# Both halves of a block's values in one place, and the value loads right behind it: an attention and feed-forward kernel on one Trainium2 core

## The chip, the cores and the metric

The kernel runs on one core of a Trainium2 chip. The metric is the device time in microseconds, the median of the runs. One execution was also taken by the hardware profiler; its page and its trace are quoted below. Engines are named as there: PE is TensorE's matrix multiplication and PEld its weight load, DVE is VectorE, ACT is ScalarE, POOL is GpSimd, SP is SyncE, which here only issues DMA transfers.

## The reference

Eight batches of attention with twelve heads, 448 positions and 64 values per head. Two 12 x 12 matrices mix the heads, one ahead of the softmax and one behind it. A feed-forward layer with a gate of its own follows. All in fp32.

```python
scores = scale * np.matmul(q, k.transpose(0, 1, 3, 2))
scores = np.einsum('bhij,hg->bgij', scores, w_pre)
scores = scores - np.max(scores, axis=-1, keepdims=True)
attn = np.exp(scores)
attn = attn / (np.sum(attn, axis=-1, keepdims=True) + 1e-09)
attn = np.einsum('bhij,hg->bgij', attn, w_post)
attn_out = np.matmul(attn, v)              # (8, 12, 448, 64)
x = attn_out.transpose(0, 2, 1, 3).reshape(3584, 768)
h = x @ w_in                               # 768 -> 2048
out = (h - np.tanh(h)) @ w_out             # 2048 -> 768
```

## The kernel before

The kernel has two stages. The first, some 940 us of the profiled execution, is the attention; beside it the weights of the feed-forward layer, which arrive as pairs of 32-bit words, are converted in small steps (`narrow_steps`, 56 chunks) and stored to DRAM (`ws`). The second stage is the feed-forward layer, and the change does not touch it.

**Blocks and places.** A batch's 448 positions are cut into four blocks of 120, 120, 120 and 88, so there are 32 blocks. A block is worked off in groups of ten positions times twelve heads (120 rows), which makes 45 groups in a batch and 360 in all. The main loop takes two groups at a time; each round is a *place* `p`, and there are 180. Every place does the following, in this order on TensorE:

- `premix(p)` (L504 to L509): mixes the heads of the scores of two groups, into `ps_p`. The first group is multiplied in fp32, the second in three passes of split operands (`th`, `tl`).
- jobs that the table `todo[p]` lists: `prep_k` (L407, transposes keys), `prep_q` (L433, transposes queries), `values` (L586, attention times values), `scores` (L467, queries times keys).
- `mix(p - 1)` (L549): the second mixing of heads for the two groups of the place before, into `ps_o`.

Beside that, DVE takes the maxima (`mx`, L519) and ACT the exponentials (`e`, L521) of the place; ACT scales `wpost` by the sums (`wr`, L537) and copies the mix of the place before from PSUM into the tile `at` (L558, L565). `scores` leave as `s` (L473, three copies on ACT, one on DVE); two places later SP's `gather` (L488) brings groups of them as `t` into the shape that `premix` needs. POOL and DVE split `t` (L496, L497).

**Values.** `values(i, t)` multiplies block `i` for six heads, half `t` of 0 and 1. Its 24 matmuls run as pairs in the two column halves of the array (`j * D`), over four chunks of keys. The result leaves by DVE copies (L604) into the tile `x`, and behind the second half of every other block SP stores `x` to DRAM (`xs`). The values of a batch come in three loads of four heads (`vr`, three buffers, `load_v`); half 0 reads the first and a part of the second, half 1 the rest. All of `prep_k`, `prep_q`, `values` and `scores` take their PSUM banks from one pool of four, `ps_m`: one bank for each job of the first three kinds, four for a pair of `scores`.

**What sets the order.** On each engine the instructions run in the order in which the program is written (`in_order`). The table is filled ahead of the loop: a list `halved` has, for each block, three jobs of scores ("s", four heads each) and two of values ("v"), each with its earliest and latest place; one is put into each place, the one that is due first, and kinds take turns if that makes nobody late. A block's values can begin two places after its last group's. `prep_q` stands one place ahead of the scores that need it. `load_k` and `load_v` go into the places at fixed distances from a block's start. A load that is put into a place is issued by SP at the beginning of the next one, behind that place's two gathers (`issue`); the stores of converted weights (`ws`) and the loads of the next chunk (`cr`) come after these, in the same SP queue.

Of the kernel before, what the change touches and what calls it, by code (L numbers as in the profile page):

```python
# [148 lines left out]
def kernel_body(  # L149
# [179 lines left out]
    with ExitStack() as st:  # L329
# [377 lines left out]
        NG = len(groups)  # L707
# [5 lines left out]
        NPL = NG // 2  # L713
# [8 lines left out]
        def at_place(p, *job):  # L722
            todo[p].append(job)

        halved = []
        for i in range(len(blocks)):

            f0, f1, f2 = first[i : i + 3]
            if i + 1 < len(blocks):
                lo = max(0, (f0 - 1) // 2 - 1)  # L730
                hi = f1 // 2 - 3
                for x in range(0 if i else 1, 3):
                    e = lo + 2 * x if lo + 4 <= hi else lo + (hi - lo) * x // 2
                    halved.append((e if i else x - 1, hi, "s", i + 1, x))
            for x in range(2):
                halved.append(((f1 - 1) // 2 + 2, f2 // 2 + 1 if f2 < NG else NPL + 7, "v", i, x))
        at_s, p, kind = {}, 0, None
        while halved:
            ready = sorted((x for x in halved if x[0] <= p), key=lambda x: (x[1], x[3:]))
            if ready:  # L740
                x = ready[0]
                assert p <= x[1], (p, x)

                other = [y for y in ready if y[2] != kind]
                if x[2] == kind and other and x[1] > p + 1:
                    x = other[0]
                halved.remove(x)
                _, _, kind, i, n = x
                if kind == "s":
                    at_s[i, n] = p  # L750
                    for hp in (2 * n, 2 * n + 1):
                        at_place(p, scores, i, hp)
                else:
                    at_place(p, values, i, n)
            p += 1
        for i, (b, m) in enumerate(blocks):
            p0 = first[i] // 2
            if i + 2 < len(blocks):
                p = at_s[i + 2, 0] - 1
                at_place(p, prep_q, i + 2, 0)  # L760
                at_place(p, prep_q, i + 2, 1)
                if i + 3 < len(blocks):
                    at_place(p + 1, load_q, i + 3)
            if b and m == 0:
                for hq in range(NP // 2):
                    at_place(p0 + 4 + hq, load_v, b, hq)
        for b in range(1, B):
            p, o, done = first[blocks.index((b - 1, 1))] // 2 - 1, 0, []
            for hq in range(3):
                if hq == 2:  # L770

                    p = max(p, done[0] + 1)
# [81 lines left out]
    for n in range(N):  # L854
        b, f = n // NF, n % NF
# [49 lines left out]
```

## Time and profile before

| | us |
|---|---|
| median of 3 runs | 1884.85 (1882.71 to 1889.16) |
| the profiled execution | 1890.93 |
| its span, first to last instruction | 1889.2 |

| in the profiled execution | |
|---|---|
| mean granted TensorE clock | 0.996 |
| DMA over the span | 371.92 MB, mean 197 GB/s |
| a value load (`vr`) | 24 of 448.0 KB |
| a key load (`kr`) | 23 of 448.0 KB |
| a gather (`t`) | 342 of 210.0 KB, 16 of 189.0 KB on SP |
| a store of attention output (`xs`) | 8 of 720.0 KB, 8 of 624.0 KB |

Times in the lines of the profile are microseconds from the span's start unless marked ns. In rows of the timeline the first number is the start and the second the length of the merged run of like instructions; an fp32 matmul of the program stands there as two instructions. In rows of groups the numbers behind the first bar are busy time and mean ns of one, and behind the second the idle time of the engine just before them and what ended it. In rows of waits the numbers are us in total, times, and the longest. SPq is SP's queue of DMA issues. Lengths of matmuls overlap, so starts are compared rather than lengths.

### The profile page before, as it was taken

How to read it: one execution, taken by the hardware profiler on the slowest of the kernel's cores; microseconds unless marked ns; L12 is line 12 of the kernel's file. 1: busy time of each engine (PE TensorE's matmuls, PEld its weight loads, DVE VectorE, ACT ScalarE, POOL GpSimd, SP SyncE). 2: the span in 40 equal slices, each digit the busy share in tenths (PEclk: the TensorE clock that was granted, in tenths of full speed). 3: DMA queues.
4: the chain of work that ended last, by engine and by line, in shares of the span. 5: the costliest groups of instructions: out<-in, count | busy, mean ns of one | idle time of the engine just before them, and what ended most of it. 6: DMA issues, size and time to landing. Idle time of an engine off the chain costs nothing.

```text
span 1889.2 us, 35293 instructions
## 1 busy us (share of the span) xinstructions
PE 1856.8 (98%) x13122; PEld 1525.3 (81%) x13122; DVE 1187.3 (63%) x2462; ACT 1136.4 (60%) x2510; POOL 455.3 (24%) x401
## 2 busy tenths in 40 slices
PE   8999999999999999999999999999999999999998
PEld 5777887777877787877788888888888888888887
DVE  5676766767776676766456556556556556556555
ACT  5787887878888788788633433443443443443433
POOL 1344444444444345444200000000000000010000
PEclk8999999999999999999999999999999999999999
DMA  6667658676575857656565566555655655655650
GB/s 150 182 186 207 188 164 220 182 199 198 176 217 168 207 180 207 191 162 195 204 259 211 197 227 215 212 213 207 215 213 209 218 214 202 220 214 199 216 198 34
DMA packets 232219, 371.92 MB, mean 197 GB/s; under 512 B 98928, under 2 KB 206960, under 8 KB 217712
## 3 DMA queue, kind: packets, MB, share of 16 engines
q1 hardware_dynamic: 231740, 369.24, 60.4%
q8 instruction: 104, 1.70, 0.4%
q14 instruction: 67, 0.55, 0.1%
q10 hardware_dynamic: 308, 0.43, 0.1%
HBM read 245.37 MB, written 47.19 MB: 155 GB/s over the span
## 4 chain that ended last, share of the span: by engine, by line
PE 87%; DMA 5%; ACT 3%; issue 1%; DVE 1%; SPq 1%; POOL 0%; ACTq 0%; DVEq 0%; POOLq 0%
PE ps_o L549 14%; PE ps_h L260 8%; PE ps_h L256 8%; PE ps_h L255 8%; PE ps_m L586 7%; PE ps_q L467 6%; PE ps_p L504 6%; PE ya L299 5%; PE ya L302 5%; PE ya L300 5%; DMA t<-s 3%; PE yb L300 3%; PE yb L302 3%; PE yb L299 3%; PE ps_p L508 2%; PE ps_p L507 2%
## 5 line engine op out<-in xcount | busy, mean ns | idle before, releaser
L549 PEld LDWEIGHTS ps_o<-wr,e 120*112 120x112 f32 (+1 forms) x2880 | 307.2, 177 | 50.7 <-issue 29.9
L549 PE MATMUL ps_o<-wr,e 120*112 120x120 f32 (+1 forms) x2880 | 340.5, 271 | 4.8 <-ACT wr L537 4.8
L519 DVE TENSOR_REDUCE mx<-ps_p 120x1 f32<-120x448 f32 x360 | 218.8, 623 | 139.1 <-PE ps_p L504 139.0
L497 POOL TENSOR_TENSOR tl<-t,th 120x448 fp32r<-120x448 f32 x179 | 204.8, 1144 | 392.0 <-DVE th L496 258.9
L287 ACT CAST gh<-r 128x512 fp32r<-128x512 f32 (+1 forms) x113 | 69.7, 617 | 378.2 <-DVE r L280 378.2
L256 PE MATMUL ps_h<-xl,w 128*128 128x512 f32 x672 | 263.8, 393 | 0.5 <-POOL pad L222 0.5
L255 PE MATMUL ps_h<-xh,w 128*128 128x512 f32 x672 | 263.8, 393 | 0.0
L521 ACT ACTIVATE e<-ps_p,mx 120x448 f32<-120x448 f32 x360 | 226.0, 637 | 34.7 <-DVE mx L519 34.2
L245 POOL TENSOR_TENSOR xl<-rx,xh 128x512 fp32r<-128x512 f32 x38 | 56.5, 1488 | 742.5 <-ACT xh L244 742.5
L558 ACT COPY at<-ps_o 112x960 f32<-112x960 f32 x156 | 154.5, 990 | 113.9 <-PE ps_o L549 113.0
L299 PE MATMUL ya<-w,gh 128*128 128x512 f32 x448 | 177.4, 396 | 2.5 <-ACT gh L287 2.5
L276 DVE SCALAR_TENSOR_TENSOR r<-qa,ps_h 128x512 f32<-128x512 f32 (+1 forms) x113 | 77.2, 683 | 160.3 <-ACT t L273 160.3
L300 PE MATMUL ya<-w,gh 128*128 128x512 f32 x448 | 177.2, 396 | 0.0
L302 PE MATMUL ya<-w,gl 128*128 128x512 f32 x448 | 176.4, 394 | 0.5 <-DVE gl L288 0.5
L260 PE MATMUL ps_h<-xh,w 128*128 128x512 f32 x672 | 172.9, 392 | 0.0
L504 PE MATMUL ps_p<-t,wpre 120*120 120x448 f32 x360 | 165.7, 542 | 3.6 <-ACT e L521 3.0
L586 PE MATMUL ps_m<-at,vr 112*64 112x120 f32 (+1 forms) x3072 | 162.8, 263 | 0.9 <-ACT at L558 0.9
L270 ACT ACTIVATE u<-ps_h 128x512 f32<-128x512 f32 (+1 forms) x113 | 67.2, 595 | 155.7 <-PE ps_h L260 155.7
L586 PEld LDWEIGHTS ps_m<-at,vr 112*64 112x64 f32 x3072 | 149.2, 138 | 13.5 <-issue 4.1
L260 PEld LDWEIGHTS ps_h<-xh,w 128*128 128x128 f32 x672 | 126.4, 188 | 27.9
L256 PEld LDWEIGHTS ps_h<-xl,w 128*128 128x128 f32 x672 | 126.4, 188 | 24.8 <-POOL pad L222 0.9
L255 PEld LDWEIGHTS ps_h<-xh,w 128*128 128x128 f32 x672 | 126.5, 188 | 23.8
(99 smaller groups left out, 3621.8 us busy)
## 6 DMA issues: line engine op xcount, KB each, us to landing
w<-ws SPq DMA_DIRECT2D x112, 1536.0 KB
t<-s SPq DMA_DIRECT2D x342, 210.0 KB
cr<-in_moe_w_in_dram SPq DMA_DIRECT2D x24, 512.0 KB
cr<-in_moe_w_out_dram SPq DMA_DIRECT2D x32, 384.0 KB
vr<-in_v_dram SPq DMA_DIRECT2D x24, 448.0 KB
out_dram<-ob SPq DMA_DIRECT2D x28, 384.0 KB
kr<-in_k_dram SPq DMA_DIRECT2D x23, 448.0 KB
qr<-in_q_dram SPq DMA_DIRECT2D x23, 360.0 KB
```

The lines of the kernel that those rows point to most:

```text
L255: nc.tensor.matmul(ph, wh[:, fs], xh, start=(c == 0), stop=False)
L256: nc.tensor.matmul(ph, wh[:, fs], xl, start=False, stop=False)
L260: nc.tensor.matmul(ph, wl[:, fs], xh, start=False, stop=(c == NK - 1))
L299: nc.tensor.matmul(y, gh[:, tok], wh[:, es], start=first, stop=False)
L300: nc.tensor.matmul(y, gh[:, tok], wl[:, es], start=False, stop=False)
L302: nc.tensor.matmul(y, gl[:, tok], wh[:, es], start=False, stop=last)
L497: eng.tensor_sub(tl[:n, :], x[:n, :], raw(th[:n, :]))
L504: nc.tensor.matmul(pa[:n, :], wpre[:n, :n], tg.pop(2 * p)[:n, :], start=True, stop=True)
L519: nc.vector.tensor_reduce(out=mx[:n, :], in_=ps[:n, :], axis=AX.X, op=ALU.max, negate=True)
L521: nc.scalar.activation(e[:n, :], ps[:n, :], AF.Exp, bias=mx[:n, :], scale=1.0, accum_out=zs[:n, 0, j : j + 1])
L549: nc.tensor.matmul(ps[:CP, j, c * GP : (c + 1) * GP], e[:n, c * CP : (c + 1) * CP], wr[:n, j, :], start=True, stop=True,)
L586: nc.tensor.matmul(pv[j * D : (j + 1) * D, r, :n], vt[:, j, c, :], ats[i][:, c, 2 * hp + j, :n], start=(c == 0), stop=(c == NC - 1),)
```

## The change

The planner lists one job of values per block instead of two, and that job puts both halves into one place. The three value loads of a new batch are put into the three places behind the one with the values of the block before (`at_v`), instead of the fourth to sixth place after the batch's start.

```diff
-            for x in range(2):
-                halved.append(((f1 - 1) // 2 + 2, f2 // 2 + 1 if f2 < NG else NPL + 7, "v", i, x))
+            halved.append(((f1 - 1) // 2 + 2, f2 // 2 + 1 if f2 < NG else NPL + 7, "v", i, 0))
...
                 else:
-                    at_place(p, values, i, n)
+                    at_v[i] = p
+                    for t in range(2):
+                        at_place(p, values, i, t)
...
             if b and m == 0:
+                p = at_v[i - 1] + 1
+                assert p + 4 < at_v[i], (p, at_v[i])
                 for hq in range(NP // 2):
-                    at_place(p0 + 4 + hq, load_v, b, hq)
+                    at_place(p + hq, load_v, b, hq)
```

The number of instructions on each engine stays as it is, and the scores stay in their places but for three, which move up by one (places 46, 91 and 136 to 45, 90 and 135). On TensorE this is the first block's values, with its two halves in places 7 and 9 before (`ps_m` from `at` and `vr`, 24 matmuls a half). The first piece is place 7, where keys of the next batch are transposed as well:

```order
 L509 MATMUL ps_p<-tl,wph 120x448
 L407 MATMUL ps_m<-ident,kr 128x112 x8
-L586 MATMUL ps_m<-at,vr 64x120 x24
+L586 MATMUL ps_m<-at,vr 64x120 x48
 L549 MATMUL ps_o<-wr,e 112x120 x8
 L504 MATMUL ps_p<-t,wpre 120x448
```

Both halves stand in a row now. The second piece is place 9 on TensorE:

```order
 L509 MATMUL ps_p<-tl,wph 120x448
 L433 MATMUL ps_m<-ident,qr 128x88 x6
-L586 MATMUL ps_m<-at,vr 64x120 x24
 L549 MATMUL ps_o<-wr,e 112x120 x8
 L504 MATMUL ps_p<-t,wpre 120x448
```

Only the transposes of queries are left between premix and mix. Over the 180 places, those with queries alone go from 1 to 23 and those without a job from 17 to 26. On SP these are the loads of the sixth batch's values, with the seventh's keys (`kr`), before the change, at about 621 to 638 us of the profiled execution:

```order
L359 DMA vr<-in_v_dram 112x4x256
L359 DMA xs_61<-x 768x1x208
L488 DMA t<-s 120x1x448 x2
L359 DMA qr<-in_q_dram 88x12x64
L359 DMA vr<-in_v_dram 112x4x256
L359 DMA kr<-in_k_dram 112x16x64
L488 DMA t<-s 120x1x448 x2
L359 DMA vr<-in_v_dram 112x4x256
L359 DMA kr<-in_k_dram 112x16x64
L359 DMA ws_67<-cs 128x384
L359 DMA ws_67<-cl 128x384
```

Of the three value loads two are followed by a key load at once. The same stretch of SP with the change; the store of `x` (`xs_61`) stands two rows above the first of these:

```order
L359 DMA vr<-in_v_dram 112x4x256
L359 DMA ws_67<-cs 128x384
L359 DMA ws_67<-cl 128x384
L359 DMA cr<-in_moe_w_out_dram 128x768
L488 DMA t<-s 120x1x448 x2
L359 DMA vr<-in_v_dram 112x4x256
L488 DMA t<-s 120x1x448 x2
L359 DMA qr<-in_q_dram 88x12x64
L359 DMA vr<-in_v_dram 112x4x256
L359 DMA kr<-in_k_dram 112x16x64
L488 DMA t<-s 120x1x448 x2
L359 DMA kr<-in_k_dram 112x16x64
```

One place is left in which a value load and a key load follow one another, and a pair of weight stores and a weight load now stand among the value loads.

More of the change, by code (lines that the diff above doesn't have):

```diff
@@ L734, in kernel_body @@
                     halved.append((e if i else x - 1, hi, "s", i + 1, x))
-            for x in range(2):
-                halved.append(((f1 - 1) // 2 + 2, f2 // 2 + 1 if f2 < NG else NPL + 7, "v", i, x))
-        at_s, p, kind = {}, 0, None
+            halved.append(((f1 - 1) // 2 + 2, f2 // 2 + 1 if f2 < NG else NPL + 7, "v", i, 0))
+        at_s, at_v, p, kind = {}, {}, 0, None
         while halved:
```

## The prediction

> **What bounds the kernel now.** I read the page first (busy shares, then the chain that ended last), then the busy time in stretches, then single places in the timeline.
>
> ```profile
> PE 1856.8 (98%) x13122; PEld 1525.3 (81%) x13122; DVE 1187.3 (63%) x2462; ACT 1136.4 (60%) x2510; POOL 455.3 (24%) x401
> PE 87%; DMA 5%; ACT 3%; issue 1%; DVE 1%; SPq 1%; POOL 0%; ACTq 0%; DVEq 0%; POOLq 0%
> ```
>
> TensorE is busy for 98% of the span and makes 87% of the chain. A change in the attention stage can therefore win in two ways only: fewer TensorE nanoseconds in the same work, or less of the DMA's 5% of the chain. The feed-forward stage is not touched.
>
> Where TensorE waits shows in stretches around the change of batch (columns: stretch, its length, then busy us and count of PE, PEld, DVE, ACT, POOL, granted clock, DMA share, GB/s):
>
> ```profile
> 160.00:200.00 40.00, 39.88 (x378) 32.08 (x377) 28.17 (x76) 33.16 (x83) 16.44 (x16) 1.00 0.85 234
> 280.00:320.00 40.00, 37.42 (x361) 29.88 (x357) 25.15 (x67) 30.32 (x74) 16.34 (x14) 1.00 0.93 243
> 400.00:420.00 20.00, 19.51 (x163) 15.29 (x163) 12.79 (x34) 14.25 (x38) 6.89 (x7) 1.00 0.99 234
> 520.00:560.00 40.00, 38.32 (x364) 31.16 (x364) 28.71 (x70) 31.39 (x77) 17.50 (x15) 1.00 0.82 223
> 620.00:660.00 40.00, 36.86 (x350) 29.33 (x347) 25.76 (x69) 29.32 (x75) 15.33 (x15) 1.00 0.88 222
> 740.00:760.00 20.00, 18.41 (x193) 15.01 (x192) 12.35 (x35) 13.78 (x32) 11.23 (x9) 1.00 1.03 249
> 860.00:880.00 20.00, 20.00 (x180) 15.88 (x179) 13.95 (x35) 17.13 (x44) 11.61 (x11) 1.00 0.72 198
> ```
>
> Five of the seven have TensorE idle: 2.58 + 0.49 + 1.68 + 3.14 + 1.59 = 9.5 us, at DMA shares of 0.82 to 1.03. The last one, where three value loads come but no next batch's keys, loses nothing. The SP queue and the chain say why (start us, us):
>
> ```profile
> 626.76 2.57 SPq L359 DMA_DIRECT2D vr<-in_v_dram  x1
> 629.38 2.02 SPq L359 DMA_DIRECT2D kr<-in_k_dram  x1
> 631.50 4.89 SPq L488 DMA_DIRECT2D t<-s  x2
> 637.00 0.66 SPq L359 DMA_DIRECT2D kr<-in_k_dram  x1
> 637.76 4.65 SPq L359 DMA_DIRECT2D ws<-cs  x1
> ```
>
> ```profile
> 281.59 9.28 DMA kr<-in_k_dram
> ...
> 299.19 5.97 DMA t<-s
> ...
> 625.09 6.92 DMA t<-s
> ```
>
> A key load issues in 0.66 us, yet behind value and key loads a store of a converted weight chunk keeps the queue 4.65 us and a pair of gathers 4.89 us. The chain runs through a key load that lands 9.28 us after its issue and through gathers of 6 to 7 us. So the loss is value loads, the xs store and key loads falling together, with the gathers behind them.
>
> **The change, part by part.** *(a) Second half of the values right behind the first.* 31 of the 32 blocks have a half moved. Counted over the two orders, the places with q alone go from 1 to 23 and the empty ones from 17 to 26; so 22 of the freed places keep q and 9 end up empty. The price comes from four kinds of place (start us, us; a place runs from its first L504 to the next one):
>
> ```profile
> 40.50 0.92 PE L504 MATMUL ps_p<-t,wpre 120*120 120x448 f32 x2
> 41.87 0.78 PE L433 MATMUL ps_m<-ident,qr 120*128 120x120 f32 x6
> 42.48 1.80 PE L549 MATMUL ps_o<-wr,e 120*112 120x120 f32 x16
> 44.12 0.92 PE L504 MATMUL ps_p<-t,wpre 120*120 120x448 f32 x2
> ...
> 367.74 0.92 PE L504 MATMUL ps_p<-t,wpre 108*108 108x448 f32 x2
> 369.20 2.68 PE L586 MATMUL ps_m<-at,vr 112*64 112x120 f32 x48
> 371.81 1.90 PE L549 MATMUL ps_o<-wr,e 120*112 120x120 f32 x16
> 373.55 0.92 PE L504 MATMUL ps_p<-t,wpre 120*120 120x448 f32 x2
> ...
> 398.30 0.92 PE L504 MATMUL ps_p<-t,wpre 120*120 120x448 f32 x2
> 399.82 1.90 PE L549 MATMUL ps_o<-wr,e 120*112 120x120 f32 x16
> 401.56 0.92 PE L504 MATMUL ps_p<-t,wpre 120*120 120x448 f32 x2
> ...
> 449.13 0.92 PE L504 MATMUL ps_p<-t,wpre 120*120 120x448 f32 x2
> 451.20 2.68 PE L586 MATMUL ps_m<-at,vr 112*64 112x120 f32 x48
> 453.82 1.89 PE L549 MATMUL ps_o<-wr,e 120*112 120x120 f32 x16
> 455.55 0.92 PE L504 MATMUL ps_p<-t,wpre 120*120 120x448 f32 x2
> ```
>
> A place with q alone is 44.12 − 40.50 = 3.62 us; with q and half the values 455.55 − 449.13 = 6.42. So a half on its own costs 2.80. What it costs behind another half: the 48 value matmuls run as 24 pairs side by side, each pair 120 columns like one of the 16 mixing matmuls, which in the q place take 44.12 − 42.48 = 1.64, or 0.1025 each; 24 × 0.1025 = 2.46. The other 0.34 is going in and out of the half-width form: the values take 371.81 − 369.20 = 2.61 instead of 2.46, the mixing behind them 1.74 instead of 1.64, the rest lies at the entry. It is paid once per block now instead of twice. For the 22 blocks whose old place keeps q: 22 × 0.34 = 7.5 us. An empty place takes 401.56 − 398.30 = 3.26, not 3.00, since the mix starts 1.52 after the place's start instead of 1.37, and slower; one with values 373.55 − 367.74 = 5.81. Losing a half there saves 2.55 against the 2.46 paid elsewhere: 9 × 0.09 = 0.8. Together 8.3 us less. I take the same for the blocks of 88 tokens, as going in and out does not depend on columns.
>
> [...]
>
> *(b) What the thinner places lose.* In an empty place the mix waits for ScalarE's `wr` behind its copy of the mix before:
>
> ```profile
> PE ps_o L549 <- ACT wr L537: 4.8, 8, 1.4
> ```
>
> All such waits were 4.8 us in 8 places; even if all lay in the 17 empty places, that is 0.28 each, 2.5 us for 9 more. The other end is 0. I take 1, since most empty places show none. The 22 new places with q alone shorten the time for `qh` and `ql`, which the scores of the next place read (rows of a place with q and values that starts at 332.88, and of two groups of DVE: a conversion step and the copies of the values):
>
> ```profile
> 332.88 0.92 PE L504 MATMUL ps_p<-t,wpre 120*120 120x448 f32 x2
> 335.79 0.83 ACT L446 ACTIVATE qh<-ps_m 128x360 fp32r<-128x360 f32 x2
> 336.29 0.97 DVE L448 SCALAR_TENSOR_TENSOR ql<-ps_m,qh 128x360 fp32r<-128x360 f32 x2 [0.41 <-ACT qh L446]
> ...
> L89 DVE SCALAR_TENSOR_TENSOR cr<-cm,cs 128x384 int32<-128x384 int32 (+1 forms) x56 | 38.6, 691 | 3.5 <-ACT e L521 0.5
> L604 DVE COPY x<-ps_m 128x360 f32<-128x360 f32 (+1 forms) x80 | 47.9, 634 | 26.7 <-PE ps_m L586 26.5
> ```
>
> `ql` is done 4.38 us after the place began. A place with q alone ends at 3.62 and the next one's scores start 1.37 later (40.50 to 41.87), at 4.99: a margin of 0.61, less whatever conversion step DVE has ahead. The longest such step, 0.69, is 0.1 beyond the margin; two are about 0.7. Bounds: 0 to 22 × 0.7 = 15 us; I take 2, nearer the end that the row shows. ACT's two `qh` copies (0.83) were there before, in a place 2.8 us longer; they may push its later copies, which is in the same 2.
>
> *(c) DVE, PSUM, tiles.* Nothing is added: the same copies of `x`, now two in a row. The first runs beside the second half on TensorE, the second stands where it stood. Cover is the 1.74 + 1.37 = 3.1 us of mix and premix before the next scores want a bank; in a place with k as well the four banks are all in use but free by then. Tiles `at`, `x`, `vr` come free earlier, and nobody waits for them later. Price 0; without that cover one copy's length, 0.63 us, in 14 places.
>
> *(d) The loads.* The three value loads move one or two places up on SP, and the xs store two to four (its half is done earlier), so that of three places in which value and key loads followed one another one is left or none. SP's new wait (values of the place before) is over when SP comes to it. Bounds: all 9.5 us goes, or nothing; below that, up to another 9.5 if the earlier loads hit gathers that were undisturbed. The nearest rows are 860:880 and 160:200, which lose 0 and 0.12 although they too hold three value loads (the second also two key loads and the xs store). Between the ends I take 5 us.
>
> Sum: −8.3 + 1 + 2 − 5 = −10.3 us. The profiled execution took 1890.93 us (span 1889.2 and 1.7 around it), which gives 1880.6. It is 6.1 us over the median of the runs, 1884.85, and the likeliest thing to differ between runs is the DMA waits, so in a median run there may be less to win in (d), say 4 instead of 5: 1884.85 − 9.3 = 1875.5. I predict **1875.5 us**.
>
> **Rivals.** *The loads take their delay along.* The bytes are the same: a value load of 448 KB (table of the profile) at the 222 GB/s of 620:660 is 2 us of every engine, and whichever gather follows it waits. For it: the gathers are on the same queue in both orders. Against: the two stretches that lose nothing. Then (d) is 0 and the time 1884.85 − 8.3 + 3 = 1879.6, no change that can be told. [...]
>
> *The collision goes wholly.* Then (d) is 9.5: 1884.85 − 8.3 + 3 − 9.5 = 1870.
>
> *Thin q places starve the scores* (slower). In each of the 22, `ql` comes after the third pass wants it. At 0.7 us late each it is 15.4: with (d) at 0, 1884.85 − 8.3 + 1 + 15.4 = 1893. It decides from (5.7 + 8.3 − 1)/22 = 0.6 us late per place. Against: the margin of 0.61 above. For it: the only place with q alone, at 40.50, lies ahead of the conversion, so no row shows one under load.
>
> **How the numbers follow.** 0.3% (5.7 us) is about what a measurement of this kernel can tell from no change. My forecast 0.57 (1870 to 1879), the collision wholly gone 0.13, loads that take their delay along 0.22, starved scores 0.08. Faster is the first two, 0.70; same 0.22; slower 0.08. The range of 8 in 10 leaves out the slow rival and the far end of the full relief: 1868 to 1883.
>
> **What would show it.** (a): places with k and both values near 9.0 us, q alone near 3.6, empty near 3.26; the group of value matmuls shorter in sum. (b): TensorE's waits for `wr` well under 8 us and for `ql` or `qh` hardly any. (d): the seven stretches with less than 5 us idle, and key loads landing in less than 9 us. I am wrong if scores wait in q places, or if PE idle near batch changes stays at 9 us.

## The result, and the profile after

| | before | changed |
|---|---|---|
| median of 6 runs each, us | 1886.13 (1882.05 to 1890.46) | 1899.82 (1894.22 to 1906.69) |
| ratio to before, 95% interval | | 1.0079 [1.0060, 1.0099] |
| the profiled execution, us | 1890.93 | 1900.2 (span 1898.5) |

The change makes the kernel 0.8% slower, about 14 us in the medians. 1875.5 was forecast, with a chance of 0.08 for slower.

The page of the changed kernel, busy engines and the shares of the chain:

```profile
PE 1852.2 (98%) x13122; PEld 1527.6 (80%) x13122; DVE 1199.6 (63%) x2462; ACT 1132.4 (60%) x2510; POOL 454.8 (24%) x401
PE 79%; ACT 7%; DMA 6%; issue 3%; DVE 3%; SPq 2%; POOL 1%; ACTq 0%; POOLq 0%; DVEq 0%
```

TensorE's busy time fell (1856.8 to 1852.2 us), in the direction that (a) of the prediction gives it for 31 entries fewer into the half-width form. Its share of the chain fell from 87% to 79%, and ACT's rose from 3% to 7%: something else sets the time at more places. The same seven stretches as before (stretch, length, busy us and count of PE, PEld, DVE, ACT, POOL, granted clock, DMA share, GB/s):

```profile
160.00:200.00 40.00, 39.35 (x350) 32.18 (x349) 30.05 (x78) 34.45 (x90) 17.39 (x16) 1.00 0.82 229
280.00:320.00 40.00, 37.14 (x321) 30.32 (x320) 26.78 (x66) 30.47 (x74) 16.47 (x14) 0.96 0.79 210
400.00:420.00 20.00, 19.54 (x204) 16.24 (x204) 12.67 (x32) 13.59 (x36) 6.75 (x7) 1.00 0.90 218
520.00:560.00 40.00, 37.33 (x357) 30.72 (x357) 27.91 (x64) 30.93 (x75) 17.46 (x14) 0.96 0.72 201
620.00:660.00 40.00, 38.52 (x336) 30.62 (x333) 29.36 (x76) 32.66 (x81) 17.28 (x16) 1.00 0.74 215
740.00:760.00 20.00, 13.81 (x95) 10.62 (x93) 12.60 (x30) 14.94 (x38) 9.89 (x8) 0.89 0.92 234
860.00:880.00 20.00, 18.04 (x152) 13.85 (x152) 10.01 (x33) 15.72 (x40) 6.54 (x6) 1.00 0.85 236
```

The stretches are the same in time, not in the work that falls into them, so this is a first look. TensorE now idles 0.65 + 2.86 + 0.46 + 2.67 + 1.48 + 6.19 + 1.96 = 16.3 us in them, against 9.6 before (the 9.5 of the prediction and the 0.12 of the first), although the DMA shares fell in six of the seven. And a number stands there that was 1.00 in every row before: the granted clock is 0.96, 0.96 and 0.89. The waits of TensorE (us in total, times, longest):

```profile
PE ps_m L407 <- DMA kr<-in_k_dram: 14.0, 6, 5.8
PE ps_o L549 <- ACT wr L537: 11.1, 17, 1.3
...
PE ps_q L467 <- ACT qh L446: 0.3, 1, 0.3
```

Before the change the two rows for the key transposes were these:

```profile
PE ps_m L407 <- ACT e L521: 4.3, 2, 2.8
PE ps_m L407 <- DMA kr<-in_k_dram: 3.2, 2, 1.8
```

The first of them names the exponentials `e`, but those two waits (places 7 and 142) very likely were for key loads as well. In an undisturbed place (58, before the change) the transposes begin 1.36 us behind the place's start, ahead of its `e`; and in the trace the load for place 142 landed at 753.57 us, 0.04 us ahead of that `e`, and the transposes began 0.14 us behind the landing, as they do in place 52. So the waits for keys went from some 7.5 us to 14.0, and the mix waits for `wr` 11.1 us instead of 4.8. The scores do not wait for `qh`, except once for 0.3 us.

**One late key load, closely.** These keys are transposed in place 52. TensorE around that place (start us, us; in brackets the idle time ahead and what ended it):

```profile
286.02 0.92 PE L504 MATMUL ps_p<-t,wpre 120*120 120x448 f32 x2
...
290.42 0.96 PE L407 MATMUL ps_m<-ident,kr 112*128 112x112 f32 x8 [2.86 <-DMA kr<-in_k_dram]
291.30 6.80 PE L586 MATMUL ps_m<-at,vr 112*64 112x120 f32 x96
...
299.77 0.54 PE L504 MATMUL ps_p<-t,wpre 120*120 120x448 f32 x1
```

The chain of the changed kernel has the load itself, its consumers, and the same two steps of an undisturbed place (58) for comparison:

```profile
281.03 9.25 DMA kr<-in_k_dram
...
290.42 0.96 PE ps_m L407 x8
291.37 6.74 PE ps_m L586 x96
...
322.42 0.77 PE ps_m L407 x8
323.18 5.07 PE ps_m L586 x96
```

The load lands 9.25 us after its issue, and 9.28 before the change (its row is in the prediction): unchanged. But place 52 starts 286.02 − 281.03 = 4.99 us after the issue, where it started 288.06 − 281.59 = 6.47 after it before (TensorE, before the change):

```profile
288.06 0.92 PE L504 MATMUL ps_p<-t,wpre 120*120 120x448 f32 x2
...
291.00 0.96 PE L407 MATMUL ps_m<-ident,kr 112*128 112x112 f32 x8 [1.40 <-DMA kr<-in_k_dram]
```

A key load is due in a *place*, and that place now comes sooner behind the issue. Place 142, four batches later, shows the same. SP's issue of the keys and TensorE's start of the place, before the change:

```profile
744.78 0.67 SPq L359 DMA_DIRECT2D kr<-in_k_dram  x1
```

```profile
750.59 0.54 PE L504 MATMUL ps_p<-t,wpre 120*120 120x448 f32 x1
```

The same two with the change, and on SP the two loads ahead of the keys:

```profile
743.24 2.70 SPq L359 DMA_DIRECT2D vr<-in_v_dram  x1
745.98 1.72 SPq L359 DMA_DIRECT2D cr<-in_moe_w_in_dram  x1
...
749.56 0.65 SPq L359 DMA_DIRECT2D kr<-in_k_dram  x1
```

```profile
751.21 0.54 PE L504 MATMUL ps_p<-t,wpre 120*120 120x448 f32 x1
```

From the issue of the keys to the start of their place it was 6.47 and 5.81 us in these two places; it is 4.99 and 1.65. In place 97, by the same rows, it went from 5.68 (513.37 to 519.05) to 3.86 (515.84 to 519.70). Two things took the difference, and the place two ahead of each shows both. It gave up its half of values and is shorter (place 50: 4.50 us instead of 5.16; 95: 4.01 instead of 5.16; 140: 3.58 instead of 5.16). And SP's work of a place did not get shorter with it, so the keys are issued later within it: 0.83, 0.67 and 2.69 us later behind its start, the last of these because a value load and a weight load held the queue for 4.4 us. In place 52 TensorE so waits 2.86 us instead of 1.40. Then a second price is paid: 5.07 us of value matmuls take 6.74, and the transposes 0.96 instead of 0.77. The busy times in steps of 2 us (columns as in the stretches above):

```profile
290.00:292.00 2.00, 1.58 (x18) 1.47 (x20) 1.13 (x3) 1.94 (x6) 2.00 (x2) 0.89 0.75 245
292.00:294.00 2.00, 2.00 (x24) 2.00 (x22) 1.01 (x2) 1.35 (x3) 1.44 (x2) 0.50 0.98 234
```

After the idle time the granted clock is 0.50 (trace: from 291.58 for 3.41 us). 2.86 of waiting, 1.67 of slow value matmuls and 0.19 at the transposes make 4.72 us, by which this place (13.75 us from L504 to L504) exceeds an undisturbed one (9.03). Place 97 loses 4.03 us (13.06) and place 142 7.93 (16.96, with the clock at 0.50 for 6.83 us). Together the three cost 16.7 us, of which 10.9 are the waits themselves (2.86, 2.23 and 5.83) and most of the rest goes with the half clock (0.50 for 3.41 us in place 97, from 523.69); before, places 52 and 142 lost 1.6 and 1.8 against the shortest of their kind, and place 97 nothing. A fourth, place 7, had lost 4.6 us before the change, with 3.41 us of half clock (from 62.41), and loses 5.6 now. In place 52 the half clock came with a wait of 2.86 us, and no low clock with the 1.40 us of before. But the length of the wait draws no sharp bound here: in place 97 a wait of 2.23 us sufficed, and the last section has a shorter one with the half clock and a longer one without it.

**Where thin places lose.** The run of places 60 to 63 has queries alone, scores, scores, nothing. TensorE's starts of places, and its mix in the empty one:

```profile
334.48 0.92 PE L504 MATMUL ps_p<-t,wpre 120*120 120x448 f32 x2
338.10 0.92 PE L504 MATMUL ps_p<-t,wpre 120*120 120x448 f32 x2
...
347.72 0.92 PE L504 MATMUL ps_p<-t,wpre 120*120 120x448 f32 x2
...
350.51 1.89 PE L549 MATMUL ps_o<-wr,e 120*112 120x120 f32 x16 [1.26 <-ACT wr L537]
```

ACT in the same time:

```profile
343.59 0.66 ACT L102 CAST cs<-cm 128x512 fp32r<-128x512 f32 x1
344.11 0.66 ACT L82 ACTIVATE cm<-cm 128x512 f32<-128x512 f32 x1
...
347.30 1.43 ACT L473 COPY s<-ps_q 120x448 f32<-120x448 f32 x3
348.56 0.75 ACT L85 ACTIVATE cr<-cr 128x512 f32<-128x512 int32 x1
349.13 1.04 ACT L558 COPY at<-ps_o 112x960 f32<-112x960 f32 x1
349.98 0.76 ACT L537 ACTIVATE wr<-wpost,zs 120x120 f32<-120x120 f32 x2
```

The place with queries alone takes 3.62 us as forecast. But ACT does three steps of the conversion here (L82, L85, L102; 0.7 us each) while the places 60 to 62 take 13.24 us instead of the 15.63 of before (from 332.88 to 348.51). It falls behind, and `wr` is 1.26 us late in the empty place, which takes 4.52 us instead of 3.26; before the change the same place took 3.61.

### The profile page after: what moved, and what is told of

Same layout as the page of the kernel before. It is cut to its first block, busy times and chain, and to the rows that moved or that the text cites. A ratio compares the mean times of both kernels' runs of the same rounds, so it can differ in the third digit from the quotient of the medians.

```text
span 1898.5 us, 35295 instructions
## 1 busy us (share of the span) xinstructions
PE 1852.2 (98%) x13122; PEld 1527.6 (80%) x13122; DVE 1199.6 (63%) x2462; ACT 1132.4 (60%) x2510; POOL 454.8 (24%) x401
## 4 chain that ended last, share of the span: by engine, by line
PE 79%; ACT 7%; DMA 6%; issue 3%; DVE 3%; SPq 2%; POOL 1%; ACTq 0%; POOLq 0%; DVEq 0%
PE ps_o L549 11%; PE ps_h L260 8%; PE ps_h L256 8%; PE ps_h L255 8%; PE ps_m L586 8%; PE ya L299 5%; PE ya L302 5%; PE ya L300 5%; PE ps_q L467 4%; PE ps_p L504 4%; PE yb L300 3%; PE yb L302 3%; PE yb L299 3%; DMA kr<-in_k_dram 3%; ACT e L521 2%
## 5 line engine op out<-in xcount | busy, mean ns | idle before, releaser
L549 PE MATMUL ps_o<-wr,e 120*112 120x120 f32 (+1 forms) x2880 | 339.3, 271 | 11.4 <-ACT wr L537 11.1
L504 PE MATMUL ps_p<-t,wpre 120*120 120x448 f32 x360 | 165.6, 542 | 2.2 <-ACT e L521 1.5
L586 PEld LDWEIGHTS ps_m<-at,vr 112*64 112x64 f32 x3072 | 153.5, 141 | 10.6 <-ACT at L565 6.0
```

What stands on the lines that cost most here:

```text
L504: nc.tensor.matmul(pa[:n, :], wpre[:n, :n], tg.pop(2 * p)[:n, :], start=True, stop=True)
L549: nc.tensor.matmul(ps[:CP, j, c * GP : (c + 1) * GP], e[:n, c * CP : (c + 1) * CP], wr[:n, j, :], start=True, stop=True,)
L586: nc.tensor.matmul(pv[j * D : (j + 1) * D, r, :n], vt[:, j, c, :], ats[i][:, c, 2 * hp + j, :n], start=(c == 0), stop=(c == NC - 1),)
```

## The experiments

Each run was compared with the kernel before on the same chip; the medians of before were 1883.4, 1886.8, 1885.9 and 1887.1 us in the four sets. Three theories for the loss were open: key loads come too late because the places ahead of them are shorter; the moved value loads disturb others; the thinner places leave too little time beside the conversion.

**The value loads back.** The changed kernel with its value loads where they were.

```diff
-                    at_place(p + hq, load_v, b, hq)
+                    at_place(p0 + 4 + hq, load_v, b, hq)
```

> Both halves of the values in one place, but the value loads back at the fourth to sixth place after the batch's start. Theory A (the places ahead of the key transposes have lost a half of values each, so key loads have less time and TensorE waits for them): as slow as the changed kernel or slower, 1900 to 1910 us, waits for key loads 14 us or more, since value loads fall together with key loads again. Theory B (thin places: TensorE waits for ACT's wr): within 3 us of the changed kernel, key waits unchanged. Theory C (the moved value loads are what costs): back to the time before or better, 1878 to 1888 us, key waits about 3 us.

1902.76 us, ratio 1.0109 [1.0087, 1.0131]. TensorE's waits:

```profile
PE ps_m L407 <- DMA kr<-in_k_dram: 14.3, 4, 6.2
PE ps_m L586 <- DMA vr<-in_v_dram: 5.5, 3, 3.7
```

Key loads are as late as with the loads moved (14.0), and values now come late too. (A wait of 1.5 us in place 97, put down to `e`, ended 0.13 us behind the landing of its key load and belongs to the first row as well.) From the issue of the keys to the start of their place it is 3.93, 3.55 and 3.78 us here, 2.0 to 2.5 less than before the change, though the loads stand in the places where they stood then. So the merging alone makes the keys late, and moving the value loads is not what costs. It rather helps, by the waits for `vr`; in the medians the two versions' intervals overlap.

**Keys three places earlier** (the first two loads of a batch):

```diff
-                at_place(p, load_k, b, hq)
+                at_place(p - 3 if hq < 2 else p, load_k, b, hq)
```

> The changed kernel with the first two key loads of each batch three places earlier; the transposes stay. A: TensorE's waits for key loads fall from 14 us to under 3, the granted clock stays at 1.00 near the batch changes, and the time falls by 12 to 16 us to 1884 to 1888. B: no more than 4 us less. C: waits move to the gathers and the time stays within 4 us.

1887.04 us, 1.0023 [1.0008, 1.0038]. The waits for keys are gone from the list, and of the 0.8% under a third is left. `wr` stays at 11.1 us, and another wait has grown:

```profile
PE ps_p L504 <- ACT e L521: 8.0, 7, 2.7
```

It was 1.5 us in the changed kernel; in the chain of this run gathers of 5.4 us stand at 732 and 740, where keys now meet the value loads.

**Values ahead of the keys within a place.** The transposes then come 5 us later.

```diff
-        rank = {prep_k: 0, prep_q: 0, values: 1, scores: 2}
+        rank = {values: 0, prep_k: 1, prep_q: 1, scores: 2}
```

> The changed kernel with the values ahead of the key and query transposes inside a place, no load moved. The key loads get 5 us more. A: waits for key loads 14 us to under 4, time 1885 to 1890. B: within 4 us of the changed kernel. C: within 4 us, waits elsewhere.

1888.45 us, 1.0032 [1.0019, 1.0045]. No wait for keys either, with the loads issued as in the changed kernel: it is the due time that decides. `wr` rose to 15.8 us.

**Conversion dealt by the width of the places**, none in those with queries alone or empty. Instead of an even rate, a place with values gets 1.6 shares of the steps and one with scores 1.0.

```diff
+            return 1.6 if values in jobs else 1.0 if scores in jobs else 0.0
...
+                conv.rate = (11 * len(chunks) + 1) * weight(p) / conv_all
```

> The changed kernel with the conversion steps of the weights dealt out by place: none in places without scores and values, 1.6 times the share of a place with scores in places with values. A: key waits as before at about 14 us, time within 4 us of the changed kernel. B: TensorE's waits for wr fall from 11 us to under 4 and the time by 6 to 8 us, to about 1893.

1896.0 us, 1.0068 [1.0043, 1.0092]. A came true, with 14.1 us for keys and an interval that overlaps the changed kernel's; B is a miss, since `wr` waits were 14.5 us in 20 places. Places with scores, which often precede an empty place, got more steps by this deal; that ACT is therefore already behind when the empty place begins is argued, not shown.

**Keys eight places earlier, with the change and without.** Eight places put the loads ahead of the value loads. The second kernel is the one before the change, with this edit alone.

```diff
-                at_place(p, load_k, b, hq)
+                at_place(max(0, p - 8) if hq < 2 else p, load_k, b, hq)
```

> The changed kernel with the first two key loads of each batch eight places earlier, where no value load stands, instead of three places, where they met the value loads. If what was left of the collision (gathers landing late around the sixth and eighth change of batch, some 12 us of TensorE idle in that run) came from keys and values together: TensorE's waits for keys under 2 us, for late gathers under 3, time 1876 to 1881 us. If bytes at the batch change are the cause wherever they stand: 1886 to 1889.

> The kernel before with the same key loads eight places earlier, values in two halves. The 9.5 us of idle near batch changes should go in the same way: 1874 to 1878 us. Its difference to the merged kernel with the same loads is then the net price of the merge alone: by the prediction's steps the merged one is 5 us faster (8.3 saved, 3 lost); if thin places lose some 10 us, the merged one is 2 us slower or the same.

With the change 1875.03 us, 0.9938 [0.9924, 0.9952]; without it 1872.61, 0.9926 [0.9913, 0.9939]. Two stretches of the first of these (columns as above), which lost 2.86 and 6.19 us in the changed kernel:

```profile
280.00:320.00 40.00, 40.00 (x415) 33.49 (x411) 30.86 (x73) 33.21 (x81) 18.89 (x15) 1.00 0.65 201
740.00:760.00 20.00, 18.69 (x190) 15.50 (x187) 16.09 (x37) 15.15 (x39) 9.75 (x8) 1.00 0.63 192
```

The idle time goes, but for 1.31 us that is a wait for `wr`, and the clock is 1.00. The kernel before gained as well, 14.2 us. Merging still does not pay, even with early keys: 2.4 us slower by the medians, with intervals that overlap. `wr` waits with the change and, in the second fence, without it:

```profile
PE ps_o L549 <- ACT wr L537: 12.0, 18, 1.3
```

```profile
PE ps_o L549 <- ACT wr L537: 3.7, 7, 1.3
```

**The same two without any conversion beside the attention.** All of it is done in one piece near the end of the stage, so that the whole time (2190.85 and 2196.17 us) says nothing; the stretch from the start of place 4 to that of place 170 does.

```diff
-        conv = Steps(narrow_steps(nc, cv, partial(dma, to=slow), chunks), 11 * len(chunks) + 1, NPL - 16)
+        conv = Steps(narrow_steps(nc, cv, partial(dma, to=slow), chunks), 0.0, NPL - 16)
```

> As the merged kernel with keys eight places early, but all conversion of the weights behind the last places but three, so that no place holds a conversion step; the time in all is far longer and tells nothing, only the stretch from place 4 to place 170 does. If thin places stall since conversion steps hold ACT and, by way of POOL, DVE: TensorE's waits for wr fall from 11 us to under 2 there, and the stretch is about 8 us shorter than with halves apart. If the chain from mix over the copy and wr to the next mix is too long by itself: waits stay at 8 to 11 us and the stretches are alike.

> The kernel before with keys eight places early and all conversion behind the last places but three, as a yardstick for the merged one: waits for wr under 1 us, and the stretch from place 4 to place 170 about 8 us longer than the merged kernel's if conversion is what stalls thin places, the same length if not.

The two ends of the stretch on TensorE, with the change and early keys and no conversion, and then the same without the change:

```profile
41.18 0.54 PE L504 MATMUL ps_p<-t,wpre 120*120 120x448 f32 x1
861.90 0.54 PE L504 MATMUL ps_p<-t,wpre 120*120 120x448 f32 x1
```

```profile
39.78 0.54 PE L504 MATMUL ps_p<-t,wpre 120*120 120x448 f32 x1
868.57 0.54 PE L504 MATMUL ps_p<-t,wpre 120*120 120x448 f32 x1
```

820.72 against 828.79 us: merged values save 8.07. TensorE is busy for 820.37 and 828.15 us of these, at a clock of 1.00, so the saving is nearly all in its own work. The other four kernels, from the same rows of their timelines:

| place 4 to place 170, us | values merged | values split | merged − split |
|---|---|---|---|
| as it is | 40.17 to 900.36: 860.19 | 44.12 to 891.49: 847.37 | +12.82 |
| keys 8 places early | 41.67 to 878.61: 836.94 | 39.06 to 871.49: 832.43 | +4.51 |
| the same, no conversion beside | 820.72 | 828.79 | −8.07 |

Read upwards, the column's steps are the account of the change in three terms: −8.1 for the merging itself, +12.6 for what it loses beside the conversion (merged places pay 16.2 us for having the conversion there, split ones 3.6), and +8.3 for late keys (23.3 against 14.9). They sum to the 12.8 us seen. The terms are taken away one after the other in this order; taken in another, they might split otherwise. The conversion took its transfers with it, so the second term is that of engines and transfers together.

Each stretch is of one execution, and that of the merged kernel with early keys was the slowest of its six (1878.56 us). By the medians the differences are 13.7 as it is and 2.4 with early keys, and the terms +10.5 and +11.3 instead of +12.6 and +8.3. So each of the two is known to two or three us, and which is the larger stays open.

TensorE's time in the same stretches, busy and idle, tells where the terms come from:

| TensorE busy and idle, us | values merged | values split |
|---|---|---|
| as it is | 832.78 and 27.41 | 833.36 and 14.01 |
| keys 8 places early | 823.15 and 13.79 | 828.51 and 3.92 |
| the same, no conversion beside | 820.37 and 0.35 | 828.15 and 0.64 |

The conversion's term is mostly idle time (10.2 of the 12.6 us). The term of late keys is 3.5 us of idle time and 4.8 us of longer busy time. The half clock is large enough for the latter: in its four stretches in the changed kernel TensorE is busy for 17.29 us, in the one before the change for 3.42, and by an estimate from the clock of 0.50 at most a half of that is lost.

**Which engine loses beside the conversion.** Four runs with the change and keys eight places early. First the deal again, with 2.2 shares for places with values, 0.8 with scores and 0.35 for the rest:

> Merged values, keys eight places early, conversion steps dealt out by place: 2.2 shares where values stand, 0.8 with scores, 0.35 in places with neither. Without conversion the merged stretch from place 4 to 170 is 16 us shorter. If the steps in thin places and in the runs of scores between them are what stalls: waits for wr from 11 us to under 6, time 1875 to about 1868. If any step beside the attention costs the same wherever it stands: 1873 to 1877.

1872.53 us, 0.9927 [0.9909, 0.9945]: 2.5 us less by the medians, with intervals that overlap, and less than expected; `wr` waits are 9.9 us instead of 12.0. Then ACT's three conversion steps go to DVE (the first of three lines):

```diff
-    nc.scalar.mul(m, m, 2.0**-112)
+    nc.vector.tensor_scalar(m, m, 2.0**-112, None, op0=ALU.mult)
```

> Merged values, keys eight places early, the three conversion operations of ACT on DVE instead. If ACT falls behind by its conversion operations (0.6 us a place) and the mix then waits for wr: waits for wr from 11 us to under 4, time about 1866. If DVE, held up by POOL's adds, is what comes late: waits stay or grow, since DVE gets 0.6 us a place more, and the time is 1875 or more.

1869.5 us, 0.9910 [0.9893, 0.9927]; 5.5 us less than with them on ACT, and the waits for `wr` fall from 12.0 to 7.5 us. ACT's load is part of the cause, and not all of it. Then POOL's three steps to DVE, ACT's left in place (one of three lines):

```diff
-    nc.gpsimd.tensor_tensor(out=m, in0=m, in1=u.bitcast(F32), op=ALU.add)
+    nc.vector.tensor_tensor(out=m, in0=m, in1=u.bitcast(F32), op=ALU.add)
```

> Merged values, keys eight places early, the three conversion operations of POOL on DVE instead. If DVE's cast of t waits for POOL's 1.3 us adds (a cast took 1.37 us instead of 0.39 until such an add was over) and maxima, exponentials and wr come late behind it: waits for wr from 11 us to under 5, time about 1867, casts over 0.6 us nearly gone. If ACT's operations are the cause: waits stay near 11 us and the time near 1875, or worse by DVE's added 0.7 us a place.

1885.37 us, 0.9999 [0.9984, 1.0014]: 10 us worse, `wr` waits 17.4. It removes one disturbance (see the last section) and puts a larger load on DVE, so it does not settle DVE's share. Last, both the steps off ACT and the deal:

> Merged values, keys eight places early, ACT's conversion operations on DVE, and the steps dealt out 2.2, 0.8 and 0.35. What is left in thin places is some 8 us over the stretch without conversion. If it is DVE, now with those operations, that comes late there: waits for wr from 7 us to under 4, time 1864 to 1867. If the order of the two edits' gains is not additive since both remove the same waits: 1868 to 1870.

1877.23 us, 0.9947 [0.9929, 0.9965]: a miss, 8 us worse than without the deal, although `wr` waits are down to 5.7 us. The stretch from place 4 to place 170 is 6.5 us longer (835.22 against 828.74), and 5.1 of them lie in place 98, one with scores, which takes 9.75 us instead of 4.61:

```profile
516.95 0.99 PE L467 MATMUL ps_q<-kk,qh 64*120 64x448 f32 x3 [1.62 <-DVE kk L419]
```

DVE begins to write this `kk` at 516.28, behind two conversion steps in a row: L82, which was ACT's, took 1.40 us instead of the usual 0.42, and L83 1.50 instead of 0.42. Both lie beside steps of POOL (L96, L98). Behind the wait the clock is 0.50 for 6.83 us. So heaped steps make DVE late here; that holds for this one place of the profiled execution.

**The kernel before with the same two edits.** The values split as before, keys eight places early, ACT's steps on DVE:

> The kernel before, values in two halves, with keys eight places early and the conversion's ACT operations on DVE: the yardstick for the merged kernel with the same two edits (1869.5 us). If the merge loses only by what ACT's conversion operations and late keys cost in thin places, this one gains less from the edit than the merged one's 5.5 us, 0 to 3, and is slower than it: 1870 to 1873. If the merge has another price, this one is the faster: 1864 to 1868.

1868.9 us, 0.9901 [0.9885, 0.9917], 18 us under before; `wr` waits:

```profile
PE ps_o L549 <- ACT wr L537: 1.6, 2, 1.4
```

With merged values the same edits gave 1869.5. The edit gained 3.7 us here, and the time lies between the two that were expected, so it decides for neither. The stretches from place 4 to place 170 are 828.47 and 828.74 us: with ACT relieved the merging comes out even, where the structure alone would give it 8. TensorE idles 0.32 us in the split kernel's stretch and 6.54 in the merged one's, of which 5.9 are waits for `wr`.

## Why the prediction was wrong, step by step

*(a) The merging itself: right.* −8.3 was forecast, −8.07 measured in the pair of runs without conversion, 7.78 of it in TensorE's busy time. An undisturbed place with keys and both halves took 9.03 us ("near 9.0"), with queries alone 3.62, an empty one 3.26 (median of the 26, from the starts of their L504). The blocks of 88 positions were priced like those of 120, and the medians of the places bear it out: before the change a half of theirs cost 5.77 − 3.62 = 2.15 us with queries beside it, and with the change the second half behind the first 6.98 − 5.16 = 1.82, 0.33 less; for the blocks of 120 it is 2.80 and 8.27 − 5.81 = 2.46, 0.34 less.

*(b) Thin places: mechanism partly right, size wrong.* +3 was forecast; +12.6 by the stretches and +10.5 by the medians was measured for all that the merging loses beside the conversion. The sum took +1 for `wr`, from the 4.8 us of before divided by 17 empty places, and that average was the error: it prices an empty place by the neighbours it had then. The new empty places stand in runs with other thin ones, where ACT gets the same steps of conversion in less time. With early keys, `wr` waits are 12.0 us merged and 3.7 split, which is 8.3 of the 12.6. Another 3.2 us, against 0.3, are waits of values for `at`, ACT's copy, which the prediction did not name. The other named cost, `qh` and `ql` late for the scores, and with it the slower rival, did not occur: 0.3 us in all. So the one slower rival that was priced was not the one that happened. Moving ACT's steps away took 8.2 us from the merged stretch (836.94 to 828.74) and 4.0 from the split one (832.43 to 828.47), that is 4.2 of the 12.6 us; by the medians it is 5.5 and 3.7, so 1.8. Of the other 8.4, some 6 us are idle time of TensorE, nearly all for `wr`. Why `wr` is late with ACT relieved is open; DVE has the steps then.

*(c) DVE, PSUM, tiles: 0, and nothing speaks against it.* No wait of TensorE in the list is for a bank held by `x`.

*(d) The loads: wrong in sign, and the step that turned the forecast.* −5 was forecast; +8.3 by the stretches and +11.3 by the medians was measured. This miss alone makes the sum −8.3 + 3 + 8.3 = +3; that of (b) alone makes it −8.3 + 12.6 − 5 = −0.7. The argument counted which loads fall together on SP, and spacing them was taken for a gain. It did reduce the DMA share (0.93 to 0.79 in 280:320), and the key load behind still landed in 9.25 us. What it left out is the deadline: (a) shortens the places ahead of a key load's transposes, SP's work in them stays, and a load that had no slack (9.28 us to landing, its place 6.47 us behind the issue) became later for its user by just that. The prediction held both numbers, the 9.28 us landing and the 2.55 us that each freed place loses, and never put one against the other. Its bounds of (d) did allow a loss of up to 9.5 us, but for gathers that were undisturbed, not for keys. Nor did its prices contain a change of clock, since the clock was 1.00 in all seven rows; the half clock in place 7 of the kernel before (3.41 us from 62.41) lay outside them. Its second sign of being wrong, idle time near the changes of batch that does not fall, is the one that came true. That DMA waits are what differs most between runs, for which the sum took 4 instead of 5 in a median run, was the author's estimate; no run shows it.

Its bound was too small as well: 9.5 us, the idle time in the seven stretches, was taken as all there was to win. Early keys gave the unchanged kernel 14.2 us in the median and 14.9 in the stretch.

The rival in which loads take their delay along was right that the bytes are no faster (9.25 us to landing for the keys of place 52, 9.28 before); it put the price at 0, not below.

## What to carry to other kernels

Where a load's due time is a position in the program, cutting the work between issue and use is the same as issuing it later. Before such a change, compare for each load the time from issue to landing with the time from issue to first use, and take off the latter what the change saves; where it goes under, move the issue first. A wait can also bring the half clock: in place 52 it came behind the wait of 2.86 us, and the values took 1.67 us more. And price a thinner slot by what all engines must still do in it and in its neighbours, not by the mean of slots that are thin today.

## What the runs showed of the hardware that was not expected

- A wait of just under 3 us cost over half as much again in clock: 2.86 us idle, then 3.41 us at 0.50, 1.67 us more for the same 96 matmuls. (The 0.19 at the transposes lie ahead of the low stretch.) The four low stretches of the changed kernel's attention stage last 3.41 us (from 291.58 and 523.69) or 6.83 (56.06 and 755.79), one or two times the same length. They also begin at multiples of 3.413 us from one another (69, 68 and 68 of them).
- The length of a wait alone did not decide about the clock. Waits of 2.23 and 2.32 us (places 97 and 7 of the changed kernel) had the half clock behind or within them, and so had the one of 1.62 us in the last run with the deal (6.83 us at 0.50, from 518.15). This one, from the first deal, had none; the clock is 1.00 there from 62.66 to 758.98:

```profile
289.55 0.96 PE L407 MATMUL ps_m<-ident,kr 112*128 112x112 f32 x8 [3.07 <-DMA kr<-in_k_dram]
```

On a grid of 3.413 us laid through that run's own half-clock stretches (from 59.25 and 758.98) a boundary falls at 287.94, so 1.46 us of this wait lie ahead of it and 1.61 behind. Before the change, waits of 1.59 and 1.84 us (to 753.71 and 639.34) had no half clock, though on a grid laid likewise from its half-clock stretch at 62.41 each lies nearly whole between two boundaries. What decides about the clock was not shown.
- DVE's cast of `t` usually takes 0.39 us, and 1.37 us where POOL is at an addition (the changed kernel; start us, us):

```profile
338.92 1.30 POOL L98 TENSOR_TENSOR cm<-cm,cr 128x512 f32<-128x512 f32 x1
...
339.10 1.37 DVE L496 CAST th<-t 120x448 fp32r<-120x448 f32 x1
```

It ends 0.25 us after POOL does. In this trace the 24 casts over 0.6 us all lie beside one of POOL's steps L96, L98 and L104 and end 0.24 to 0.26 us after it, while none beside no step of POOL takes over 0.40. With POOL's steps on DVE the mean of the group of casts is 391 ns, where it was 483 with early keys alone:

```profile
L496 DVE CAST th<-t 120x448 fp32r<-120x448 f32 (+1 forms) x180 | 70.4, 391 | 25.9 <-DMA t<-s 25.1 <-issue 0.8
```

That edit was still dearer than the long casts, 1885.4 us against 1875.0.
